# The last megabyte of a zero fill, written by two memory-to-memory copies of few rows

## The chip, the cores and the metric

The kernel runs on one core of one Trainium2 chip. The metric is the device time in microseconds (us) of one execution. Three runs of the kernel before took 816.27, 816.36 and 816.81 us, a median of 816.36.

## The reference

One step of decoding through an attention layer with a key and value cache and a gated feed-forward layer, and the gradients of all its inputs. The part that decides how much is written is the cache:

```
W = min(4096, max(256, Sk // 4))          # Sk = 32768, so W = 4096
k = jnp.repeat(k_cache[:, :, Sk - W:, :], rep, axis=1)
v = jnp.repeat(v_cache[:, :, Sk - W:, :], rep, axis=1)
...
_out, _vjp = jax.vjp(_f, A_x, A_k_cache, A_v_cache, A_wq, A_wo, B_w_gate, B_w_up, B_w_down)
_grads = _vjp(grad_out)
```

The caches have 8 heads of 32768 positions of 256 bfloat16 values. Only the last 4096 positions are read, so the gradient of the first 28672 positions of every head is zero. The gradients of the two caches are the outputs out_2 and out_3, 134 MB each, and seven eighths of them are zeros that the kernel must write.

## The kernel before, in words

The kernel has two kinds of work. The first is the arithmetic for the 8 heads: loads of the key and value windows, scores, softmax, moments, then the backward products and the non-zero last eighth of out_2 and out_3, along with the gradients of the weights. All loads and stores of this kind are issued on GpSimd's queue (named IO in the code, L607 and L477 for the stores), and it is spread over the whole kernel.

The second kind is the zero fill, which the change touches. SyncE issues it (named FILL in the code). L54 and L56 first load two small rows. L58 sets a tile of zeros in SBUF, 128 partitions of 8192 bfloat16 values, 16 KB in each partition. The loop at L59 and L60 runs over the 8 heads and the two outputs, which makes 16 regions of 14,680,064 bytes. L61 cuts a region in 128 x 7 rows of 16 KB, and L62 writes it with one DMA in which each partition of the tile is sent seven times:

```
reg = o[0, g, 0:Sk - W, :].rearrange("s d -> (s d)").rearrange("(p n f) -> p n f", p=128, f=ZW)
FILL.dma_start(out=reg, in_=zeros[:].unsqueeze(1).to_broadcast([128, NZ, ZW]))
```

The 16 DMAs are written in the order head 0 of out_2, head 0 of out_3, head 1 of out_2, and so on; the last is head 7 of out_3. They stand on SyncE one after the other. The first waits for the zeros. From the seventh on, each waits for the semaphore of the transfer eight places before it, since eight semaphores are used in turn. No other engine waits for a fill; the program's end (L635) waits for all of them and for the last stores of GpSimd's queue.

The DMA engines, sixteen of them, serve both queues. A fill DMA leaves one closing packet of 4 bytes per engine that it used, which raises its semaphore.

Of the kernel before, what the change touches and what calls it, by code (L numbers as in the profile page):

```python
# [16 lines left out]
G = 8  # L17
Dh = 256
W = 4096
# [3 lines left out]
Sk = 32768  # L23
# [6 lines left out]
HF = F // 2  # L30
ZW = 8192
NZ = (Sk - W) * Dh // (128 * ZW)


K_SLOT = [5, 6, 7, 5, 6, 7, 5, 7]
# [5 lines left out]
def kernel(  # L41
# [4 lines left out]
    FILL = nc.sync  # L46
# [10 lines left out]
    zeros = const.tile([128, ZW], bf16)  # L57
    V_.memset(zeros[:], 0.0)  # L58
    for g in range(G):  # L59
        for o in (out_2, out_3):  # L60
            reg = o[0, g, 0:Sk - W, :].rearrange("s d -> (s d)").rearrange("(p n f) -> p n f", p=128, f=ZW)  # L61
            FILL.dma_start(out=reg, in_=zeros[:].unsqueeze(1).to_broadcast([128, NZ, ZW]))  # L62


    S = const.tile([128, NS, SLOT], bf16)
# [494 lines left out]
    for g in range(G):  # L560
# [36 lines left out]
        for c in range(T // 2):  # L597
            d_ps = bps.tile([128, 2, 2, Dh], f32, tag="d2", bufs=2)
            for i in range(2):
                t = 2 * c + i  # L600
                k, a = t // 8, t % 8
# [38 lines left out]
```

## Time and profile before

| What | Value |
|---|---|
| median of 3 runs | 816.36 us |
| the profiled execution's own time | 816.48 us |
| its span, first to last instruction | 814.7 us |
| busy share of TensorE (matmul), VectorE, ScalarE, GpSimd | 62%, 46%, 20%, 5% |
| bytes moved by the DMA engines | 338.66 MB, mean 416 GB/s |
| zero fills on SyncE, from issue to landing (median) | 149.7 us for 14336 KB |
| stores of GpSimd's queue from SBUF tile S, from issue to landing (median) | 29.5 us for 2048 KB |

The profile is of one execution. Its times are microseconds from the span's start. The engine rows give busy time, and the DMA row the mean busy share of the sixteen DMA engines in 40 equal slices. Queue q1 is SyncE's, q0 is GpSimd's. The time from issue to landing of a fill is long since several fills are queued at once.

### The profile page before, as it was taken

Reading aid. Unit: us, or ns where it says so; the run is one execution under the profiler, and the core shown is the slowest. Engines: PE = TensorE matmul, PEld = TensorE weight load, DVE = VectorE, ACT = ScalarE, POOL = GpSimd, SP = SyncE. Lnnn points to the kernel's source line nnn. Section 1 sums busy time; section 2 is a strip of 40 time slices with the busy share of each in tenths; the row PEclk is TensorE's granted clock in tenths of the full one; section 3 lists DMA queues with packets and bytes.
Section 4 is the critical chain, followed back from the end, with each engine's and each line's share of the span. In section 5 each row is a group of like instructions: output and inputs, shape, how many; then the busy total and the mean of one; then the engine's idle time right before and its main releaser. Section 6 shows DMA issues by size and latency. Waiting matters only on the chain.

```text
span 814.7 us, 12155 instructions
## 1 busy us (share of the span) xinstructions
PE 504.1 (62%) x4991; PEld 301.7 (37%) x4991; DVE 374.4 (46%) x1149; ACT 165.0 (20%) x261; POOL 40.4 (5%) x75
## 2 busy tenths in 40 slices
PE   3559969999566947062995562597597848263200
PEld 3445646666434524031983421243143313010000
DVE  4128837776451644028733470754553626253200
ACT  0230211221101000001012231243343424142100
POOL 3000000000000001000001000001000010000000
PEclk9959878999785969565556555555555555555555
DMA  8999999999999999999999999999999999999993
GB/s 344 430 423 427 430 428 429 425 428 426 430 417 426 415 424 420 428 429 431 426 427 429 409 415 421 431 423 422 404 430 425 425 413 423 421 425 427 424 427 170
DMA packets 24573, 338.66 MB, mean 416 GB/s; under 512 B 1251, under 2 KB 1317, under 8 KB 4677
## 3 DMA queue, kind: packets, MB, share of 16 engines
q1 hardware_dynamic: 14596, 234.88, 68.3%
q0 software_dynamic: 9920, 103.00, 30.2%
q8 instruction: 39, 0.64, 0.3%
q14 instruction: 18, 0.14, 0.0%
HBM read 57.28 MB, written 280.59 MB: 415 GB/s over the span
## 4 chain that ended last, share of the span: by engine, by line
issue 59%; DMA 17%; PE 11%; DVE 4%; POOL 3%; ACT 1%; POOLq 0%; DVEq 0%
DMA S<-in_A_wo_dram 4%; DMA Rt<-in_A_wq_dram 4%; DMA out_dram<-Mt 3%; PE dq_ps L453 3%; DMA S<-in_A_k_cache_dram 3%; DMA S<-in_A_v_cache_dram 2%; PE MT L322 2%; POOL out_dram L477 1%; POOL S L79 1%; DVE Rt L423 1%; POOL out_dram L607 1%; PE dh_ps L159 1%; PE d_ps L602 1%; PE tr L568 1%; PE t L413 1%
## 5 line engine op out<-in xcount | busy, mean ns | idle before, releaser
L602 PE MATMUL d_ps<-R,Mt 32*128 32x512 bf16 x256 | 124.4, 612 | 94.4 <-DVE S L212 93.6
L322 PE MATMUL MT<-Rt,S 128*128 128x512 bf16 x512 | 156.8, 391 | 21.1 <-DMA S<-in_A_v_cache_dram 19.9
L318 DVE TENSOR_SCALAR Rt<-S,pf 128x256 bf16<-128x256 bf16 x512 | 117.8, 283 | 32.0 <-PE acc L329 17.3
L212 DVE CAST S<-d_ps 128x512 bf16<-128x512 f32 x128 | 86.8, 689 | 57.1 <-ACT S L210 43.9
L210 ACT CAST S<-d_ps 128x512 bf16<-128x512 f32 x128 | 75.1, 587 | 171.6 <-PE d_ps L602 171.6
L266 PE MATMUL tr<-ident_bf,S 128*128 128x128 bf16 x512 | 52.5, 267 | 44.5 <-DMA S<-in_A_k_cache_dram 41.2
L602 PEld LDWEIGHTS <-Mt 32*128 32x128 bf16 x256 | 23.2, 113 | 148.1 <-issue 146.7
L325 PEld LDWEIGHTS <-S 128*128 128x128 bf16 x512 | 49.9, 98 | 62.7 <-issue 6.6
L568 PE MATMUL tr<-ident_bf,S 128*128 128x128 bf16 x512 | 68.8, 304 | 3.5 <-ACT Mt L210 3.5
L329 PE MATMUL acc<-ones_bf,Rt 128*128 128x1 bf16 x1024 | 61.8, 163 | 0.0
L568 PEld LDWEIGHTS <-S 128*128 128x128 bf16 x512 | 48.5, 135 | 28.0 <-issue 27.8
L266 PEld LDWEIGHTS <-S 128*128 128x128 bf16 x512 | 41.4, 121 | 42.9 <-DMA S<-in_A_k_cache_dram 41.7
L210 ACT COPY Rt<-tr 128x1024 bf16<-128x1024 bf16 x32 | 32.4, 1012 | 84.7 <-PE tr L266 84.3
L325 PE MATMUL acc<-pT_all,S 128*128 128x2 bf16 x512 | 49.1, 165 | 0.0
L329 PEld LDWEIGHTS <-Rt 128*128 128x128 bf16 x1024 | 44.5, 96 | 0.0
L212 DVE COPY Rt<-tr 128x1024 bf16<-128x1024 bf16 x32 | 22.1, 690 | 48.5 <-PE tr L266 47.0
L210 ACT COPY Mt<-tr 128x1024 bf16<-128x1024 bf16 x32 | 32.4, 1014 | 56.3 <-PE tr L568 29.2
L322 PEld LDWEIGHTS <-S 128*128 128x128 bf16 x512 | 32.0, 97 | 21.7 <-DMA S<-in_A_v_cache_dram 20.4
L331 ACT COPY Mt<-MT 128x512 f32<-128x512 f32 x8 | 4.7, 586 | 164.8 <-PE MT L322 145.4
L573 PEld LDWEIGHTS <-Mt 128*128 128x128 bf16 x512 | 19.9, 108 | 36.7 <-DVE Mt L212 13.7
L573 PE MATMUL dp<-doT,Mt 128*128 128x2 bf16 x512 | 22.6, 168 | 12.3 <-DVE Mt L212 10.5
L212 DVE COPY Mt<-tr 128x1024 bf16<-128x1024 bf16 x32 | 22.0, 686 | 16.4 <-PE tr L568 11.3
(182 smaller groups left out, 435.1 us busy)
## 6 DMA issues: line engine op xcount, KB each, us to landing
out_dram<-zeros SPq DMA_DIRECT2D x16, 14336.0 KB, 149.7
out_dram<-S POOLq DMA_DIRECT2D x16, 2048.0 KB, 29.5
S<-in_A_v_cache_dram POOLq DMA_DIRECT2D x11, 2048.0 KB, 35.6
S<-in_A_k_cache_dram POOLq DMA_DIRECT2D x8, 2048.0 KB, 28.0
out_dram<-Mt POOLq DMA_DIRECT2D x6, 896.0 KB, 22.3
S<-in_A_wq_dram POOLq DMA_DIRECT2D x1, 3584.0 KB, 14.7
S<-in_A_wo_dram POOLq DMA_DIRECT2D x2, 1792.0 KB, 35.4
out_dram<-Mt POOLq DMA_DIRECT2D x3, 1024.0 KB, 35.7
```

The source lines that it names most:

```text
L79: IO.dma_start(out=dst, in_=cache[0, g, Sk - W:, :].rearrange("(p t) d -> p t d", t=T))
L210: S_.copy(out=out, in_=in_)
L212: V_.tensor_copy(out=out, in_=in_)
L266: P_.transpose(tr[:, i, dh, :], Xw[:, 4 * q + i, dh * 128:(dh + 1) * 128], ident_bf[:])
L318: V_.tensor_scalar(out=pk[:, i, h, :], in0=K[:, t, :], scalar1=pf[:, t, h:h + 1], scalar2=None, op0=ALU.mult)
L322: P_.matmul(MT[:, hf, :], lhsT=Vv[:, t, hf * 128:(hf + 1) * 128], rhs=pk[:, i, :, :].rearrange("p h d -> p (h d)"), start=(t == 0), stop=( ...
L325: P_.matmul(acc[:, 2 * hf:2 * hf + 2], lhsT=Vv[:, t, hf * 128:(hf + 1) * 128], rhs=pT_all[:, g, t, :], start=(t == 0 and hf == 0), stop=(t ...
L329: P_.matmul(acc[:, 4 + 2 * h + dk:5 + 2 * h + dk], lhsT=pk[:, i, h, dk * 128:(dk + 1) * 128], rhs=ones_bf[:, 0:1], start=False, stop=(t == ...
L453: P_.matmul(dq_ps[:, 2 * h + dk:2 * h + dk + 1], lhsT=Mt[:, h // 2, hf, c0:c0 + 128], rhs=doT_f[:, 2 * h + hf:2 * h + hf + 1], start=(hf = ...
L568: P_.transpose(tr[:, i, dh, :], Vw[g][:, 4 * q + i, dh * 128:(dh + 1) * 128], ident_bf[:])
L573: P_.matmul(dp[:, 4 * q + i, :], lhsT=xt[:, i, dh, :], rhs=doT[:, 4 * g + dh:4 * g + dh + 3:2], start=(dh == 0), stop=(dh == 1))
L602: P_.matmul(d_ps[:, i, :, :].rearrange("p w d -> p (w d)"), lhsT=rows[32 * k:32 * k + 32, a, :], rhs=R[32 * k:32 * k + 32, :], start=True, ...
```

## The change

The last of the 16 regions (head 7 of out_3) is no longer written by one DMA but by four, which a list gives as (rows, pieces, values of a piece). The first writes 12 MiB of the region as before, with six pieces of 16 KB for each partition. The second writes 1 MiB from the tile of zeros, 8 KB for each partition. The third and the fourth write the last 1 MiB, and their source is no longer the tile: they read from the first region of out_2 (head 0), which the first fill has set to zero. The third has 4 rows of 4 pieces of 64,256 bytes (257,024 bytes a row), and in its source the rows are five pieces apart. The fourth has 5 rows of one piece of 4096 bytes, two pieces apart in its source. Together they are 1,048,576 bytes. The other 15 regions are written as before, and the instructions of the other engines stay in their order.

```diff
+LAST_FILL = [(128, NZ - 1, ZW), (128, 1, ZW // 2), (4, 4, 32128), (5, 1, 2048)]
...
-            reg = o[0, g, 0:Sk - W, :].rearrange("s d -> (s d)").rearrange("(p n f) -> p n f", p=128, f=ZW)
-            FILL.dma_start(out=reg, in_=zeros[:].unsqueeze(1).to_broadcast([128, NZ, ZW]))
+            flat = o[0, g, 0:Sk - W, :].rearrange("s d -> (s d)")
+            last = g == G - 1 and o is out_3
+            a = 0
+            for p, n, f in LAST_FILL if last else [(128, NZ, ZW)]:
+                dst = flat[a:a + p * n * f].rearrange("(p n f) -> p n f", p=p, f=f)
+                if p == 128:
+                    src = zeros[:, 0:f].unsqueeze(1).to_broadcast([128, n, f])
+                else:
+                    src = out_2[0, 0, 0:Sk - W, :].rearrange("s d -> (s d)")[0:p * (n + 1) * f]
+                    src = src.rearrange("(p n f) -> p n f", p=p, f=f)[:, 0:n, :]
+                FILL.dma_start(out=dst, in_=src)
+                a += p * n * f
```

On SyncE, the four DMAs stand at the end in this order. The second waits for the semaphore of the 9th fill, the third for that of the 10th and the fourth for that of the 11th; the first waits, as the whole fill did, for the 8th.

More of the change, by code (lines that the diff above doesn't have):

```diff
@@ L60 @@
         for o in (out_2, out_3):
-            reg = o[0, g, 0:Sk - W, :].rearrange("s d -> (s d)").rearrange("(p n f) -> p n f", p=128, f=ZW)
-            FILL.dma_start(out=reg, in_=zeros[:].unsqueeze(1).to_broadcast([128, NZ, ZW]))
+            flat = o[0, g, 0:Sk - W, :].rearrange("s d -> (s d)")
[10 more added lines that the diff above has]
+                a += p * n * f
+            assert a == (Sk - W) * Dh
     S = const.tile([128, NS, SLOT], bf16)
```

## The prediction

> **What bounds the kernel now.** I read the DMA parts of the page first, because the slices of part 2 show no compute engine near full and the DMA row full in 38 of 40 slices.
>
> ```profile
> span 814.7 us, 12155 instructions
> ...
> DMA  8999999999999999999999999999999999999993
> ...
> q1 hardware_dynamic: 14596, 234.88, 68.3%
> q0 software_dynamic: 9920, 103.00, 30.2%
> ...
> HBM read 57.28 MB, written 280.59 MB: 415 GB/s over the span
> ```
>
> The reader is to see that q1, SyncE's queue of zero fills, takes 68.3% of the sixteen DMA engines' time and GpSimd's q0 30.2%: 98.5% together. So the span is the work of the DMA engines, and only its end matters for this change. The count on q1 tells how fills are cut: 16 fills x 896 rows of 16 KB, 16 closing packets for each fill (one per DMA engine), and one row with one closing packet for each of the two small loads, 14336 + 256 + 4 = 14596. So a fill uses all sixteen engines, 56 rows each, and a DMA of one row used one engine.
>
> Next the windows at the end (us from the span's start; the last two numbers are DMA share and GB/s):
>
> ```profile
> 770.00:780.00 10.00, 0.00 (x0) 0.00 (x0) 0.00 (x0) 0.00 (x0) 0.00 (x0) 0.50 1.03 435
> 780.00:790.00 10.00, 0.00 (x0) 0.00 (x0) 0.00 (x0) 0.00 (x0) 0.00 (x0) 0.50 0.99 423
> 790.00:800.00 10.00, 0.00 (x0) 0.00 (x0) 0.00 (x0) 0.00 (x0) 0.00 (x0) 0.50 0.96 410
> 800.00:805.00 5.00, 0.00 (x0) 0.00 (x0) 0.00 (x0) 0.00 (x0) 0.00 (x0) 0.50 0.41 174
> 805.00:810.00 5.00, 0.00 (x0) 0.00 (x0) 0.00 (x0) 0.00 (x0) 0.00 (x0) 0.50 0.12 52
> 810.00:815.00 5.00, 0.00 (x0) 0.00 (x0) 0.00 (x0) 0.00 (x0) 0.00 (x0) 0.50 0.04 16
> ```
>
> No compute runs after 770 us. The DMA engines do not finish together: at 800 us most are done, and after 808 us one is left. The trace's packet records give the sixteen closing packets of the last fill: 796.9, 797.1, 799.6, 799.9, 800.0, 800.0, 800.6, 800.7, 803.1, 803.2, 803.6, 803.6, 805.0, 807.6, 807.7 and 813.1 us. I call the first thirteen the usual engines, the next two late, the last one the straggler. The last store of q0 is closed by 798.0, so fills alone end the kernel. The straggler's last nine rows follow each other every 0.607 us though all others are idle: 16 KB in 0.607 us is its own pace (27.0 GB/s), not a share of anything. After its closing packet 1.6 us pass to the span's end, and 1.8 us lie around the span (816.48 in the profiled execution).
>
> Last, SyncE's queue, to see whether issuing could be late: its last entry in the timeline (start, us), and its waits at the end (us in total, times, longest):
>
> ```profile
> 640.99 53.22 SPq L62 DMA_DIRECT2D out_dram<-zeros  x1
> ```
>
> ```profile
> SPq L635 <- DMA out_dram<-S: 66.5, 1, 66.5
> SPq L635 <- DMA out_dram<-zeros: 52.7, 2, 44.8
> ```
>
> The last fill has been issued by 694.2, 119 us before it is closed; after that SyncE only waits for transfers to land.
>
> **The change, part by part.**
>
> *Issue and waits.* SyncE issues 19 transfers for 16. The shortest issue of a fill took 0.6 us; three more are some 2 us in a cover of 119 us, and would show only if that cover went. The new transfers wait for the semaphores of earlier fills (the 8th to the 11th, the last of them closed by 536.6 us), and the zero region that is copied was closed at 68.1 us. Nothing but the program's end is queued behind them on SyncE, so these waits cost nothing. No instruction moves on the other engines.
>
> *Removed.* The last 1 MiB no longer goes over sixteen engines: 65,536 B each, four rows at 0.607 us, so every engine's fill ends 2.43 us earlier. For the straggler this is 813.1 - 2.43 = 810.65. Eight rows of 8 KB per engine take the place of four of 16 KB, the same bytes; I put that at nothing (packets of 8 KB of instructions had a median of 0.309 us, about half of a row), and one more closing packet of 9 ns.
>
> *Added.* 4 rows x 257,024 B. Source and target are both cut in four rows that do not join, so I take one row per engine, as with the one-row loads: four engines get 15.69 times a 16 KB row each, and up to five get 4 KB more. The Trainium skill ("DMA: Bandwidth & Descriptors", section on why a DMA increments its semaphore by 16) says the same, that a transfer from SyncE uses the largest count up to 16 which divides both outer dimensions, on the lowest-numbered engines. The trace does not number the engines, so which finishing times these four have is open: 13 chances in 16 for each to be a usual one. For four of the usual the latest is around 803.6 (the twelfth of thirteen), and at most 805.0.
>
> *The price of a copied row* is the open one. No transfer here goes from memory to memory. Nearest below: a fill row, 0.607 us for 16 KB, if reading and writing the memory go side by side. Nearest above: 1.208 us for the same row, which 31 of the 14336 fill rows took (1.20 to 1.225), where I read two transfers as sharing one path; so it would be if an engine's reads and writes of the memory share one. [...] A price below the fill row I exclude, since the straggler alone goes no faster. I take 1.208: a copy passes the memory's side twice for each byte, and the row nearest to two uses of one path is this one. Then one row costs 15.69 x 1.208 = 18.95 us and the 4 KB 0.30; at the low end 9.52 and 0.15.
>
> A sentence on the skill that the sum does without: the same page (section "Latency and other measured facts") gives copies between memory tensors 214 GB/s at full rate, which over sixteen engines would be 13.4 GB/s each, by my estimate 19.2 us for a row. No run so far shows it.
>
> *The sum.* The four end at 803.6 - 2.43 + 18.95 + 0.30 = 820.4, the straggler at 810.65. The end moves from 813.1 to 820.4, +7.3 us: span 822.0, own time 823.8. The median of the runs lies 0.12 under the profiled execution: **823.7**.
>
> **The rivals.**
>
> *R1: the copy goes at the pace of a fill.* Then the four end at 803.6 - 2.43 + 9.67 = 810.8, level with the straggler at 810.65; the end comes 2.2 us earlier, and 2.43 at most: 813.9 to 814.1. At 805.0 for the latest it would be 812.2 and 815.5. It decides below 0.74 us per 16 KB (the 11.9 us between 803.6 - 2.43 and 813.1, over 15.94 rows). [...] It ends on the faster side.
>
> *R2: that pace, with a late engine among the four.* 807.7 - 2.43 + 9.67 = 814.9, +1.8: 818.2.
>
> *R3: the straggler is one of the four.* It gets the copies on top: 813.1 - 2.43 + 9.67 = 820.3 (823.6) or, at 1.208, 829.9 (833.2). Against it: one chance in four, and the change's rows would have to fall just there.
>
> *R4: the rows are cut again over all engines.* Then nothing moves but some closing packets: 816.4.
>
> **How the numbers follow.** Forecast 0.43, R1 0.36, R2 0.08, R3 0.09, R4 0.04. The forecast's own range: latest usual engine 800.0 to 805.0 gives 820.1 to 825.1. The range over all reaches from R1's best, 813.7 with some room, to 826; left out are R3 at the high price and a late engine at it (827.8), some 1 in 10. Faster by over 0.2% (1.6 us, about what a measurement can tell from no change) is R1 but for its 805.0 end, 0.33; within 0.2% that end, R4 and the lower edge of R2, 0.09; slower the rest, 0.58.
>
> **What would show it.** In the changed profile: on q1 about 14,642 packets if each row is four packets; 58.3 MB read from memory in place of 57.28; after 801 us the DMA share near 0.25 (four engines of sixteen) for some 10 us or more, at some 54 GB/s written, where before it fell from 0.41 to 0.04. The copies' packets of 64,256 B show the price directly: 4.7 us each by the forecast, 2.4 by R1. The fill's other closing packets should come 2.4 us earlier. The forecast is wrong if a copy packet takes under 2.9 us, if the four engines are not usual ones, or if more than four carry the rows.

## The result and the profile after

The changed kernel took 818.76 us in the median of 7 runs (816.46 to 820.62), the kernel before 816.45 (816.16 to 816.81). The ratio is 1.0026, interval 1.0016 to 1.0037: slower by 2.3 us, where 7.3 were forecast. The profiled execution took 819.03 us, with a span of 817.2.

The span, the DMA row, the queues and the memory's bytes, from the page of the changed kernel:

```profile
span 817.2 us, 12158 instructions
...
DMA  8999999999999999999999999999999999999992
...
q1 hardware_dynamic: 14642, 234.88, 68.1%
q0 software_dynamic: 9920, 103.00, 30.1%
...
HBM read 58.33 MB, written 280.59 MB: 415 GB/s over the span
```

The DMA engines are still full up to the last slice. The 14,642 packets on q1 are the forecast count, and so is the megabyte more that is read. The copy is cut as expected: sixteen packets of 64,256 B, four in each of four rows.

The windows at the end of the same execution (DMA share and GB/s last):

```profile
790.00:800.00 10.00, 0.00 (x0) 0.00 (x0) 0.00 (x0) 0.00 (x0) 0.00 (x0) 0.50 0.84 353
800.00:805.00 5.00, 0.00 (x0) 0.00 (x0) 0.00 (x0) 0.00 (x0) 0.00 (x0) 0.50 0.40 166
805.00:810.00 5.00, 0.00 (x0) 0.00 (x0) 0.00 (x0) 0.00 (x0) 0.00 (x0) 0.50 0.25 107
810.00:815.00 5.00, 0.00 (x0) 0.00 (x0) 0.00 (x0) 0.00 (x0) 0.00 (x0) 0.50 0.07 31
```

From 790 to 800 us the share is lower than before (0.84 for 0.96): twelve engines got less. From 805 to 810 it is 0.25, twice what it was, and from 810 to 815 little more than one engine is left (one in sixteen is a share of 0.0625, and one engine moves 27 GB/s). The GB/s fit the share as they did before the change, 107 at a quarter of the engines. Had a copied row moved at half an engine's pace, a quarter of the engines would have shown some 54.

The packet records (the trace's start, duration and size of each packet) say which engine is last. A packet starts 3 or 4 ns before the one ahead of it on its engine ends, so the packets of the last microseconds can be strung into one chain for each engine. The five chains that carry copies are, in us:

| last fill row ends | four packets of 64,256 B | 4 KB packet | end |
|---|---|---|---|
| 798.4 | 9.47 | 0.16 | 808.0 |
| 798.7 | 9.47 | 0.16 | 808.3 |
| 800.7 | 9.53 | 0.16 | 810.4 |
| 806.2 | 9.47 | 0.16 | 815.8 |
| 810.7 | none | 0.16 | 810.9 |

The last line is the straggler: 813.1 - 2.43 = 810.65 was forecast for it. The line above it sets the end, since the copies hold that engine for 9.63 us after its last fill row.

The copies cost one thing more. The second DMA of the last region leaves eight rows of 8 KB on each engine, 128 in all. Of these, 116 took about 0.309 us. The other twelve are the last three on each of the four engines that carry a copied row, and they took 0.56 to 0.61 us. On the engine that ends last this is 0.86 us together. Without it, that engine's fills would have ended at 805.3, which is 807.7 - 2.43: one of the two late engines of before.

SyncE's timeline after 640 us (start, us), and its waits at the end (us in total, times, longest):

```profile
582.62 141.42 SPq L72 DMA_DIRECT2D out_dram<-zeros  x3
724.08 35.22 SPq L72 DMA_DIRECT2D out_dram<-out_dram  x2
```

```profile
SPq L647 <- DMA out_dram<-zeros: 51.6, 3, 39.6
SPq L647 <- DMA out_dram<-out_dram: 4.8, 1, 4.8
```

The last wait is new: when all fills from the tile have landed, SyncE waits 4.8 us more for the copies, the stretch from 810.9 to 815.8. The issues end at 759.3 us where they ended at 694.2 before. The copies' first packets started at 798.4 at the earliest, so 39 us of cover are left.

### The profile page after: what moved, and what is told of

Its sections match the earlier page's. It is cut to its first block, busy times and chain, and to the rows that moved or that the text cites. A ratio compares the mean times of both kernels' runs of the same rounds, so it can differ in the third digit from the quotient of the medians.

```text
span 817.2 us, 12158 instructions
## 1 busy us (share of the span) xinstructions
PE 505.7 (62%) x4991; PEld 303.0 (37%) x4991; DVE 374.0 (46%) x1149; ACT 164.8 (20%) x261; POOL 40.4 (5%) x75
## 3 DMA queue, kind: packets, MB, share of 16 engines
q1 hardware_dynamic: 14642, 234.88, 68.1%
## 4 chain that ended last, share of the span: by engine, by line
issue 58%; DMA 16%; PE 11%; DVE 4%; POOL 3%; ACT 1%; POOLq 0%; DVEq 0%
DMA S<-in_A_wo_dram 4%; DMA Rt<-in_A_wq_dram 4%; DMA out_dram<-Mt 3%; PE dq_ps L465 3%; DMA S<-in_A_k_cache_dram 3%; DMA S<-in_A_v_cache_dram 2%; PE MT L334 2%; POOL out_dram L489 1%; POOL S L91 1%; DVE Rt L435 1%; POOL out_dram L619 1%; PE dh_ps L171 1%; PE d_ps L614 1%; PE tr L580 1%; PE t L425 1%
## 5 line engine op out<-in xcount | busy, mean ns | idle before, releaser
L585 PEld LDWEIGHTS <-Mt 128*128 128x128 bf16 x512 | 20.1, 109 | 36.3 <-DVE Mt L224 13.4
L585 PE MATMUL dp<-doT,Mt 128*128 128x2 bf16 x512 | 22.7, 168 | 11.9 <-DVE Mt L224 10.1
```

The costliest lines, as they stand in the source:

```text
L585: P_.matmul(dp[:, 4 * q + i, :], lhsT=xt[:, i, dh, :], rhs=doT[:, 4 * g + dh:4 * g + dh + 3:2], start=(dh == 0), stop=(dh == 1))
```

## The experiments

**The theory after the result.** A copied row moves at the engine's own pace, 64,256 B in 2.37 us, which is 0.605 us for 16 KB. The end is late because one of the first four engines is late by itself. **Rivals:** each extra DMA has a fixed cost; or the copies' reads slow the other engines in proportion to their bytes; or the price per row differs from execution to execution.

In all kernels but the last the list of the last region is edited, in the form (rows, pieces, values of a piece); entries of 128 rows come from the tile. Two of the kernels change a few lines more, which their diffs show. The first four were measured on one chip (816.51 us for the kernel before), the last four on another (816.54).

### Six small copies that number the engines

```diff
-LAST_FILL = [(128, NZ - 1, ZW), (128, 1, ZW // 2), (4, 4, 32128), (5, 1, 2048)]
+LAST_FILL = [(128, NZ - 1, ZW), (128, 1, 7920), (2, 1, 1024), (3, 1, 1024), (4, 1, 1024), (5, 1, 1024), (8, 1, 1024), (12, 1, 1024)]
```

> The last 70 KB of the last region are copied by six small DMAs of 2, 3, 4, 5, 8 and 12 rows of 2 KB; all else of that region comes from the tile of zeros. Each DMA engine closes as many small rows as its number allows, which gives the engines their numbers. Theory (the late end comes from a late engine among the first four, each copied row at the engine's own pace): three more DMAs cost nothing, 816.2 to 816.7; one of the first four engines ends its fills near 807.6 us, the straggler at 813 is the fifth (it showed one 4 KB row in the changed kernel). Rival (each extra DMA at the end has a fixed cost of some 0.8 us): 818 to 821.

Measured: 817.18 us, against 816.51 before on the same chip, ratio 1.0008 (0.9999 to 1.0017). That is half a microsecond above the theory's 816.7, and the rival with 0.8 us per DMA wanted 818 at least. The last region takes eight DMAs here, seven more than before and four more than in the changed kernel (the expectation says three), so the 0.67 us would be some 0.1 us for each: a cost of 0.8 us is out, a small one is not. The last four engines, by their chains:

| last fill row ends | small rows carried | so its number is | end |
|---|---|---|---|
| 806.0 | 2 | sixth to eighth | 806.2 |
| 806.4 | 2 | sixth to eighth | 806.6 |
| 807.2 | 4 | fourth | 807.6 |
| 813.7 | 3 | fifth | 814.0 |

An engine that carries four of the six small rows is in the copies of 4, 5, 8 and 12 rows and not in those of 2 and 3: it is the fourth, if the engines of a small copy are always among those of a larger one; the counts over all engines fit this, as two engines carry six rows and one each five, four and three. By the same count the straggler is the fifth. So the four rows of the change just miss the straggler and take in the late fourth. That the sets are nested agrees with the Trainium skill ("DMA: Bandwidth & Descriptors", on why a DMA increments its semaphore by 16), by which such a DMA runs on the lowest-numbered engines.

### Three rows instead of four

```diff
-LAST_FILL = [(128, NZ - 1, ZW), (128, 1, ZW // 2), (4, 4, 32128), (5, 1, 2048)]
+LAST_FILL = [(128, NZ - 1, ZW), (128, 1, 5180), (3, 4, 32128)]
```

> Three copied rows of 257,024 B in place of four and the five small ones; the tile writes the rest, so every engine gives up 48 KB, 1.79 us. Theory: if the late engine is the fourth, the straggler sets the end at 813.1 - 1.79 = 811.3 and the time is 814.6; if it is one of the first three, the end is 807.7 - 1.79 + 9.5 = 815.4 and the time 818.7. Rival (the copies slow the other engines by their reads of memory, in proportion to their bytes): three quarters of +2.3, 818.1. Forecast's price of 1.208 us for 16 KB: 821 or more.

Measured: 814.84 us, ratio 0.9979 (0.9970 to 0.9988): faster than the kernel before by 1.7 us and than the changed one by some 4. The fourth engine has no row to copy here, so it ends with its fills. The windows of this kernel (DMA share and GB/s last):

```profile
800.00:805.00 5.00, 0.00 (x0) 0.00 (x0) 0.00 (x0) 0.00 (x0) 0.00 (x0) 0.50 0.53 222
805.00:810.00 5.00, 0.00 (x0) 0.00 (x0) 0.00 (x0) 0.00 (x0) 0.00 (x0) 0.50 0.18 78
810.00:815.00 5.00, 0.00 (x0) 0.00 (x0) 0.00 (x0) 0.00 (x0) 0.00 (x0) 0.50 0.01 6
```

The stretch after 810 us is nearly empty, 0.01 where the changed kernel has 0.07. In the chains the straggler ends at 811.2 (811.3 forecast) and the three rows at 809.6, 809.6 and 811.7: the last row and the straggler end half a microsecond apart, so there is little left to shift this way. Three quarters of the bytes did not cost three quarters of 2.3 us; the rival in proportion to bytes falls. The packets of the changed kernel agree: no 8 KB row of an engine without a copied row is slowed there.

### The last megabyte left out

```diff
-LAST_FILL = [(128, NZ - 1, ZW), (128, 1, ZW // 2), (4, 4, 32128), (5, 1, 2048)]
+LAST_FILL = [(128, NZ - 1, ZW), (128, 1, ZW // 2)]
...
-            assert a == (Sk - W) * Dh
```

> The last megabyte is not written at all: the third and the fourth DMA of the last region are left out. Theory (the end before is the straggler's own pace): 813.1 - 2.43, so 813.9 to 814.1, the other engines' closings 2.4 us earlier as well. Rival (the end before is set by something other than the fills' last rows, such as the stores of GpSimd's queue): under 1 us earlier, 815.5 or more.

Measured: 814.11 us, ratio 0.9971 (0.9960 to 0.9982), 2.4 us less. The straggler ends at 811.0. The closings next to the straggler's moved by other amounts (803.2 and 804.6, where the two late engines closed at 807.6 and 807.7 before), so these engines' ends vary between executions. The removal was worth what the prediction said; the change is this 2.4 us of gain and 4.7 us of copies, which together are its +2.3.

### The four rows read from the tile of zeros

```diff
-LAST_FILL = [(128, NZ - 1, ZW), (128, 1, ZW // 2), (4, 4, 32128), (5, 1, 2048)]
+LAST_FILL = [(128, NZ - 1, ZW), (128, 1, ZW // 2), (4, 16, 8032), (5, 1, 2048)]
...
-                if p == 128:
-                    src = zeros[:, 0:f].unsqueeze(1).to_broadcast([128, n, f])
-                else:
-                    src = out_2[0, 0, 0:Sk - W, :].rearrange("s d -> (s d)")[0:p * (n + 1) * f]
-                    src = src.rearrange("(p n f) -> p n f", p=p, f=f)[:, 0:n, :]
+                src = zeros[0:p, 0:f].unsqueeze(1).to_broadcast([p, n, f])
```

> The same four rows of 257,024 B and five of 4 KB, but read from the first four and five partitions of the tile of zeros in pieces of 16,064 B, not from memory. Theory 1 (an engine's pace is all that counts, whatever the source): as the changed kernel, 818 to 819.5. Theory 2 (the four partitions lie behind one path that four engines must share, as I read the fill rows of 1.208 us): the four rows take up to four times 9.5 us, the end comes near 836 to 844 us, and the time is 840 to 848.

Measured: 842.35 us, ratio 1.0322 (1.0306 to 1.0337). The tail in the windows:

```profile
805.00:810.00 5.00, 0.00 (x0) 0.00 (x0) 0.00 (x0) 0.00 (x0) 0.00 (x0) 0.50 0.31 50
810.00:840.00 30.00, 0.00 (x0) 0.00 (x0) 0.00 (x0) 0.00 (x0) 0.00 (x0) 0.50 0.21 24
```

Here the share and the GB/s part: the engines count as busy (0.21, more than three of sixteen) and yet all together move 24 GB/s, less than one engine does alone. A packet of 16,064 B took 2.484 us in the median, 4.2 times its time at 0.605 us for 16 KB. The packets at both ends of the tail show how this grows with the engines at work: 0.60 us while one engine was reading, about 1.24 with two and 2.48 with four. So the four engines share one path out of these four partitions, 4 x 16,064 B / 2.484 us = 25.9 GB/s. The pieces are shorter here than the copied 64,256 B, but the first of them, alone, went at an engine's own pace. So the source matters a great deal, and the copy from memory is the cheap one: four engines copying at the same time took 2.37 us each for 64,256 B. The 8 KB fill rows ahead of these copies all kept about 0.309 us, so the slowing of those rows in the changed kernel goes with the source in memory.

### Rows of half the length

```diff
-LAST_FILL = [(128, NZ - 1, ZW), (128, 1, ZW // 2), (4, 4, 32128), (5, 1, 2048)]
+LAST_FILL = [(128, NZ - 1, ZW), (128, 1, 6184), (4, 2, 32128)]
```

> Four copied rows of 128,512 B, half as long, and no DMA of five rows; the tile writes the rest. Every engine gives up 32,128 B (1.19 us); a row costs 4.76 us at the engine's own pace. Theory (the fourth engine is the late one and ends its fills at 807.4 to 808.6 before the shift): it ends at 811.0 to 812.2, the straggler (the fifth) at 811.9; time 815.2 to 815.6, faster than before by about 1 us. Rival (copies cost time in proportion to their bytes by disturbing the others): half of +2.3, 817.6.

Measured: 815.51 us against 816.54, ratio 0.9987 (0.9978 to 0.9996), so faster. The fourth engine ends its fills at 806.1 and its row at 810.9; the straggler sets the end again at 812.5, 0.6 us later than expected. The rival's 817.6 is out.

### Rows of seven pieces

```diff
-LAST_FILL = [(128, NZ - 1, ZW), (128, 1, ZW // 2), (4, 4, 32128), (5, 1, 2048)]
+LAST_FILL = [(128, NZ - 1, ZW), (128, 1, 1164), (4, 7, 32128)]
```

> Four copied rows of seven pieces (449,792 B) in place of four pieces. Every engine gives up 112,448 B, 4.17 us; a row costs 16.6 us. Theory: the fourth engine ends at 807.4 to 808.6 - 4.17 + 16.6 = 819.8 to 821.0; time 823.2 to 824.5. Rival in proportion to bytes: 7/4 of +2.3, 820.5.

Measured: 822.71 us, ratio 1.0077 (1.0063 to 1.0091), 6.2 us more than before. The fourth engine starts its row at 802.7 and ends it 16.6 us later, at 819.3. The theory's lower end was 823.2, half a microsecond over. The fourth engine's last fill rows were slowed by 0.80 us here; without this its fills would have ended at 801.9, or 806.1 before the shift, where I had allowed 807.4 to 808.6. The rival's 820.5 is out on the other side.

### Five rows

```diff
-LAST_FILL = [(128, NZ - 1, ZW), (128, 1, ZW // 2), (4, 4, 32128), (5, 1, 2048)]
+LAST_FILL = [(128, NZ - 1, ZW), (128, 1, 3172), (5, 4, 32128)]
```

> Five copied rows of four pieces in place of four: the fifth engine, which the labels name as the straggler, gets a row too. Every engine gives up 80,320 B, 2.98 us. Theory: the straggler ends at 813.1 - 2.98 + 9.5 = 819.6; time 823.0. If the straggler were not the fifth engine: the late one sets the end at 808.6 - 2.98 + 9.5 = 815.1; time 818.5.

Measured: 822.98 us, ratio 1.0080 (1.0066 to 1.0094). The straggler starts its row at 810.2 and ends at 819.7, against 819.6 expected; the fourth engine ends at 814.7. The straggler is the fifth engine, here on another chip than in the run with six small copies.

### The changed kernel once more

The kernel is the changed one without an edit.

> The changed kernel once more, to see what moves its time by 4 us between executions. Theory (the fourth engine alone sets the end, and when it ends its fills varies): the profiled execution's time is the end of the fourth engine's fills plus 12.9 us (9.65 for its row and the small one, the rest for the program's end, as in its first profile: 806.17 and 819.03), whichever time it shows; the straggler ends near 810.7 in it again. Rival (the copies themselves take longer in slow executions): the copied pieces of 64,256 B take other than 2.37 us.

Measured: 818.73 us (818.03 to 819.73), ratio 1.0028 (1.0017 to 1.0040). In the profiled execution the fourth engine ends its fills at 805.70 and the execution takes 818.56: 12.86 us apart, as in the first profile (806.17 and 819.03). The straggler ends at 810.6, and the fourth engine's pieces take 2.371 us each, as before. One piece of an engine that is done by 810.3 took 2.752, which the end does not feel. So between these two executions all of the difference, 0.47 us, is the fourth engine's. For the execution of 816.46 us, of which there is no profile, the same cause is likely and not shown.

## Why the prediction was wrong, point by point

**What bounds the end: right.** The straggler's own pace, 0.607 us a row, and nothing else on its way: without the last megabyte the end came 2.4 us earlier (814.11).

**Issue and waits: no cost, as said, but my size was off.** I counted some 2 us for three more issues. SyncE was done 65 us later than before; the two issues of the copies alone took 35.2 us. That an issue is held until the transfers ahead make room is my reading, which no run tests. The queued fills covered this with 39 us to spare.

**Which engines: one row per engine, right; which of them, left open and assumed wrongly.** I took four usual engines, the latest at 803.6 before the shift. The fourth engine is a late one, at 805.3 + 2.43 = 807.7 when its slowed rows are left out. My sentence that most engines are done at 800 us was a misreading too: six of the sixteen closings lie at or before 800.0.

**The rows ahead of the copy: put at nothing, 0.86 us measured.** I took the eight rows of 8 KB as equal to four of 16 KB. They are (the last three on the late engine would have taken 0.93 us), except on the engines whose next packets are copies, where these three took 1.79 us.

**The price of a copied row: this step failed.** I put it at 1.208 us for 16 KB, "a copy passes the memory's side twice for each byte, and the row nearest to two uses of one path is this one". The sixteen pieces took 2.371 us but for one of 2.432, so 0.605 us for 16 KB, the pace of a fill row. Two of the three signs that the prediction names for being wrong came: a copy packet under 2.9 us, and an engine among the four that is not a usual one. (The price at which R1 decides is 11.9 / 15.94 = 0.75 us, not 0.74.) The reason failed too. The tile experiment shows that engines do share a path on the side of the tile, where two engines took about twice an engine's own time. The rows of 1.208 us may be such pairs, but no run shows that they are. I carried the price from the tile's side to the memory's. The straggler's own rows already gave the engine's pace, and I had no row with a cost of the memory's side. The sentence on the Trainium skill pointed the same wrong way: 13.4 GB/s for an engine was my estimate from its 214 GB/s, spread over sixteen. Four engines here moved 27.1 GB/s each (64,256 B in 2.371 us); no run copies on all sixteen, so the 214 itself is not tested.

**The sum, term by term.**

| term | forecast | measured |
|---|---|---|
| end of the fills on the latest of the four, its last rows at their usual time | 801.2 | 805.3 |
| its last fill rows slowed | nothing | 0.86 |
| its copied row | 18.95 | 9.47 |
| its 4 KB | 0.30 | 0.16 |
| end | 820.4 | 815.8 |

The misses have opposite signs, +4.1 and +0.9 against -9.5, so the forecast's side came out right by luck, with a size three times too large: with the right price alone, the same sum gives 810.8 for the four, the faster side. What happened is R2, with a price of 818.2: the pace of a fill and a late engine among the four. The slowed rows, which R2 does not have, are the 0.86 us between its end of 814.9 and the measured 815.8.

R2 had 0.08 of the chance, too little next to the 0.79 that the forecast and R1 had together. Both need four usual engines. Four engines picked at random from sixteen, of which two are late and one is the straggler, are all usual in 0.39 of the cases; they take in a late one but not the straggler in 0.36, and the straggler in 0.25. So the choice of engines was given the wrong chances even apart from the price.

**What stays open.** Why the fourth and the fifth engine are behind is not settled; no run was made for it. Nor does a run show why the last fill rows ahead of a copy from memory take twice their time.

## What to carry to other kernels

When DMA engines alone end a kernel, look at each engine's last packet, not at the mean share: the end is one engine's, and what is shifted must go to engines that are known to be early, which a few tiny copies of 2, 3, 4 and more rows can find out. Here four rows were one too many and three the version to keep (814.84 against 816.51). For a price that the trace does not have, the pace of the engine that carries it was a better guess than a doubled one whose cause had not been established.

## What the runs showed of the hardware that I had not expected

A copy from memory to memory on four engines went at 27.1 GB/s for an engine, where a fill from SBUF went at 27.0. On those four engines it also doubled the time of the last three 8 KB rows ahead of it (0.56 to 0.61 us, where 0.309 is usual), which it did not do when the same bytes came from the tile. Four engines that read four neighbouring partitions of SBUF got 25.9 GB/s together, so the same rows made the kernel 25.8 us slower than before when read from the tile (842.35 against 816.51), and 2.3 us when read from memory. The Trainium skill ("SBUF — State Buffer", "Door 1: The DMA port swizzle") has those four partitions on one port of 27.2 GB/s; the trace agrees, with 25.9.
